# Another hand-written order of all blocks in a fused delta-rule attention and MLP kernel

## The chip, the cores and the metric

The kernel runs on one core of a Trainium2 chip. Its engines are PE (TensorE, matrix multiply; PEld is its weight load), DVE (VectorE), ACT (ScalarE), POOL (GpSimd) and SP (SyncE, whose queue issues most DMAs). The metric is device time in microseconds, taken as the median of several runs. The kernel before took 590.74 us (three runs, 589.99 to 594.02).

## The reference

Four batches of eight heads (32 sequences of 768 steps, head size 48) go through a delta rule, and its result, as 3072 tokens of 384, through a two-layer MLP:

```python
k_n = k / (norm(k) + 1e-6)
for t in range(768):
    y[t]  = q[t] @ state
    v_old = k_n[t] @ state
    state = state + beta[t] * outer(k_n[t], v[t] - v_old)
x = y.transpose(0, 2, 1, 3).reshape(3072, 384)
h = x @ w_in                                  # 384 -> 2048
g = h * tanh(softplus(h))
out = g @ w_out                               # 2048 -> 384
```

q, k, v and beta are float32. The two weight matrices come as 64-bit floats and have to be turned into a high and a low 32-bit part on the chip.

## The kernel before, in words

**Attention.** The 768 steps are cut into 12 chunks of 64 (numbers 0 to 11 in the names). Two chunks make a group g (0 to 5). For each group the Gram products of k (`pg`) come from PE, ACT and DVE write them out (`d`, `at`), DVE turns them into a layout in which a triangular system can be solved (`gt`, L1461), solves it by pairs of products and sums (`pr` L1509, `gt` L1511), and turns the answer back (`d<-gt`, L1531). That last transposition of group g, `d1` for group 1 and so on, releases the products `ta2`, `ta4`, ... on PE (L1641, L1666), with which the even chunk of the group begins. Then the state goes through the chunks in series: `tb`, `pz` and `gq` (old values and products with q), `py` (result), `ps` (new state).

k of the chunks 2 and later is loaded by eight small DMAs for each chunk (`kt2`, `kt3`, `kt4`, ..., 64 KB each, L1237), and DVE transposes it in place (L1409). That transposition waits for all eight DMAs. v is loaded into `vt`, q of the first chunks into `q1`, unturned k into `xx0` and `xx1`.

**MLP.** The tokens of one chunk are one step n of the MLP: eight units `g1.n.0` to `g1.n.7` (18 matmuls each into `h`, L1888; ACT makes `e` and `g` from it in L1903 and L1904, DVE the low part of `g` in L1905) and eight units `g2.n.0` to `g2.n.7` (12 matmuls into `acc`, L1922). These 192 dense units are the filler between the steps of attention.

**Weights.** Twenty-four `ri` and thirty-two `ro` loads bring the weights; each passes through DVE (L1296, L1309, L1313, some in L1304), ACT (L1299, L1317) and, for the low part, PE (`loi`, `loo`) or an accumulating DMA issued by POOL (L1336).

**Order.** Nothing here is left to a scheduler. Each block of work is a generator with a key, and the table `TT` holds a time number for each of its pieces. `run` takes the pieces from a heap by that number and emits their instructions, on all five engines, in this order; each engine then works its own list strictly in order. So a number in `TT` decides behind which instructions another one stands on its engine, and, for loads, its place in the SP queue. `SLOT` says which buffer each tile takes. `warm` is a list of times at which dummy matmuls on a zero tile (L1949) are put on PE. SP's DMAs use eight semaphores in turn: each DMA waits until the eighth one before it has landed.

**What the change touches.** `TT`, `SLOT` and `warm`; `unit`, which copies two identity blocks into `xx0` and `xx1` each (L1220); `gram_out`, which writes out the Gram products of the first two chunks; and `out` in `early`, which does so for the groups.

Of the kernel before, what the change touches and what calls it, by code (L numbers as in the profile page):

```python
# [29 lines left out]
def bcast_in(ap, n):  # L30
# [5 lines left out]
    'loadk0': [0],  # L36
    'warm0.501': [1],
    'loadk1': [2],
    'loadi0': [3],
    'cv0': [4, 81, 110, 135, 139, 150, 151, 165, 1563],  # L40
    'warm43.6': [5],
    'loado1': [6],
    'warm36.4': [7],
    'warm0.602': [8],
    'loadi1': [9],
    'warm11.501': [10],
    'loadb': [11],
    'warm29.5': [12],
    'turn_k(0,0)': [13],
    'turn_k(0,0).0>1': [14],  # L50
    'loado2': [15],
    'turn_k(0,1)': [16],
    'turn_k(0,1).0>1': [17],
    'cv4': [18, 129, 174, 183, 209, 210, 219, 220, 714],
    'loada': [19],
    'early0': [20, 21, 24, 29, 34, 39, 44, 45, 46, 49, 50, 51, 52, 53, 57, 58, 64, 65, 66, 67, 68, 69, 70, 72, 73, 76, 84, 85, 88, 96, 97, 98, 99, 101, 102, 251, 1259],
    'turn_k(1,0)': [22],
    'turn_k(1,0).0>1': [23],
    'early0.2>1': [25],
    'early0.1>1': [26],  # L60
    'turn_k(1,1)': [27],
    'turn_k(1,1).0>1': [28],
    'loadq': [30],
    'early0.0>1': [31],
    'early0.3>1': [32],
    'loadi5': [33],
    'loadv': [35],
    'cv5': [36, 40, 176, 180, 182, 199, 200, 212, 687],
    'turn_beta()': [37],
    'cv1': [38, 55, 105, 133, 134, 145, 146, 167, 997],  # L70
    'loado14': [41],
    'warm11.602': [42],
    'warm12.101': [43],
    'turn_q0(1,)': [47],
    'turn_q0(1,).0>2': [48],
    'loado6': [54],
    'turn_q0(1,).0>1': [56],
    'turn_q0(0,)': [59],
    'warm0.6': [60],
    'warm12.3': [61],  # L80
    'warm11.903': [62],
    'loadi4': [63],
    'scale_v(0,1)': [71],
    'loado3': [74],
    'loadi2': [75],
    'warm11.603': [77],
    'warm11.702': [78],
    'warm0.5': [79],
    'warm12.1': [80],
    'ats_gq[0,1]': [82],  # L90
    'warm11.601': [83],
    'loado8': [86],
    'turn_q0(0,).0>2': [87],
    'warm12.102': [89],
    'warm12.201': [90],
    'warm11.9': [91],
    'warm30.6': [92],
    'warm30.601': [93],
    'turn_q0(0,).0>1': [94],
    'gq00': [95],  # L100
    'loado12': [100],
    'merge1': [103, 124, 270, 271],
    'merge1.0>1': [104],
    'scale_v(0,0)': [106],
    'cv12': [107, 132, 234, 258, 272, 276, 282, 283, 1487],
    'gq00.0>2': [108],
    'merge0': [109, 140, 156, 160],
    'cv2': [111, 112, 161, 162, 164, 166, 168, 202, 1269],
    'loadi9': [113],
    'cv26': [114, 127, 154, 184, 538, 542, 551, 553, 554],  # L110
    'cv8': [115, 148, 273, 274, 294, 295, 305, 306, 881],
    'loado11': [116],
    'loado10': [117],
    'gq00.0>1': [118],
    'cv17': [119, 138, 207, 394, 424, 428, 429, 431, 1435],
    'loado0': [120],
    'warm11.502': [121],
    'warm32.2': [122],
    'warm11.703': [123],
    'warm46.601': [125],  # L120
    'merge1.1>1': [126],
    'cv24': [128, 153, 228, 504, 506, 508, 511, 512, 527],
    'loado13': [130],
    'cv3': [131, 136, 137, 178, 179, 213, 235, 243, 858],
    'loadi3': [141],
    'cv19': [142, 188, 247, 415, 416, 440, 444, 455, 1325],
    'warm12.002': [143],
    'loado9': [144],
    'cv20': [147, 300, 320, 484, 485, 487, 491, 520, 550],
    'cv21': [149, 205, 206, 322, 401, 410, 411, 412, 413],  # L130
    'warm11.503': [152],
    'merge0.0>1': [155],
    'cv9': [157, 158, 175, 238, 252, 253, 254, 257, 1164],
    'merge0.1>1': [159],
    'unit(1,)': [163],
    'cv6': [169, 170, 181, 225, 226, 236, 277, 321, 902],
    'loado4': [171],
    'cv7': [172, 194, 232, 233, 242, 244, 246, 278, 442],
    'cv10': [173, 189, 237, 292, 303, 304, 317, 326, 1459],
    'loado15': [177],  # L140
    'warm40.201': [185],
    'warm11.801': [186],
    'warm12.001': [187],
    'loadi11': [190],
    'warm42.1': [191],
    'warm50.02': [192],
    'cv18': [193, 314, 318, 385, 386, 392, 393, 400, 570],
    'merge0.2>1': [195],
    'merge0.3>1': [196],
    'loado7': [197],  # L150
    'cv13': [198, 309, 327, 332, 340, 349, 354, 356, 1481],
    'ats_a[0,0]': [201],
    'cv27': [203, 316, 324, 325, 530, 543, 544, 545, 546],
    'ats_a[0,1]': [204],
    'cv23': [208, 221, 256, 341, 450, 460, 474, 475, 477],
    'ats_gq[0,1].0>2': [211],
    'warm50.04': [214],
    'ats_a[0,1].0>1': [215],
    'ats_a[0,0].0>1': [216],
    'loadi10': [217],  # L160
    'cv22': [218, 269, 374, 384, 465, 476, 480, 481, 505],
    'ats_b[0,0]': [222],
    'loado5': [223],
    'ats_b[0,0].0>1': [224],
    'ats_b[0,1]': [227],
    'loadi7': [229],
    'loadx': [230],
    'warm50.09': [231],
    'unit(0,)': [239],
    'ats_z[0,0]': [240],  # L170
    'ats_b[0,1].0>1': [241],
    'loadi6': [245],
    'ats_z[0,1]': [248],
    'ats_z[0,0].0>1': [249],
    'cv15': [250, 279, 312, 313, 328, 329, 345, 346, 433],
    'ats_y[0,0]': [255],
    'ats_z[0,1].0>1': [259],
    'cv11': [260, 265, 290, 296, 301, 302, 319, 335, 454],
    'loadp': [261],
    'loadi8': [262],  # L180
    'cv16': [263, 287, 365, 368, 369, 373, 380, 381, 471],
    'ats_gq[0,1].0>1': [264],
    'loads': [266],
    'loadk2': [267],
    'cv14': [268, 281, 289, 336, 337, 358, 359, 360, 1045],
    'merge1.2>1': [275],
    'scale_v(1,0)': [280],
    'merge1.3>1': [284],
    'warm50.11': [285],
    'warm50.13': [286],  # L190
    'warm50.14': [288],
    'scale_v(1,1)': [291],
    'ats_y[0,0].0>1': [293],
    'ats_y[0,1]': [297],
    'ats_s[0,0]': [298],
    'ats_y[0,1].0>1': [299],
    'ats_s[0,0].0>1': [307],
    'turn_q(1,0)': [308],
    'cv25': [310, 366, 367, 446, 497, 498, 503, 510, 523],
    'early1': [311, 361, 362, 364, 395, 397, 399, 405, 406, 408, 420, 421, 422, 425, 426, 434, 435, 436, 437, 438, 439, 445, 447, 449, 451, 461, 462, 464, 466, 467, 472, 473, 486, 488, 489, 493, 494, 495, 496, 499, 509, 515, 516, 517, 518, 519, 528, 529, 534, 535, 536, 537, 540, 547, 548, 549, 560, 561, 562, 563, 565, 571, 572, 573, 574, 575, 576, 580, 581, 587, 588, 598],  # L200
    'g1.0.0': [315],
    'turn_q(1,1)': [323],
    'ats_gq[1,0]': [330],
    'ats_gq[1,0].0>1': [331],
    'g1.0.0.0>1': [333],
    'ats_s[0,1]': [334],
    'ats_a[1]': [338],
    'ats_a[1].0>1': [339],
    'ats_gq[1,0].0>2': [342],
    'g1.0.1': [343],  # L210
    'g1.0.1.0>1': [344],
    'g1.0.1.0>2': [347],
    'g1.0.0.0>2': [348],
    'loadk3': [350],
    'g1.0.1.0>3': [351],
    'g1.0.0.0>3': [352],
    'g1.0.3': [353],
    'early2': [355, 478, 482, 483, 391, 539, 555, 556, 599, 607, 608, 616, 617, 619, 620, 622, 623, 627, 628, 629, 630, 634, 635, 636, 641, 642, 643, 644, 647, 648, 649, 651, 652, 653, 656, 657, 658, 665, 666, 667, 668, 669, 670, 673, 676, 677, 678, 681, 686, 688, 689, 690, 697, 698, 699, 704, 705, 706, 707, 709, 710, 711, 712, 713, 715, 717, 718, 721, 722, 724, 731, 748, 758, 763],
    'ats_s[0,1].0>1': [357],
    'early1.2>1': [363],  # L220
    'ats_b[1]': [370],
    'ats_b[1].0>1': [371],
    'g2.0.0': [372],
    'early1.3>1': [375],
    'ats_z[1,0]+s_gq[1,1]': [376],
    'ats_z[1,0]+s_gq[1,1].0>2': [377],
    'ats_z[1,0]+s_gq[1,1].0>1': [378],
    'g2.0.1': [379],
    'ats_z[1,0]+s_gq[1,1].0>3': [382],
    'ats_z[1,1]': [383],  # L230
    'g1.0.3.0>1': [387],
    'g1.0.3.0>2': [388],
    'g1.0.3.0>3': [389],
    'ats_z[1,1].0>1': [390],
    'early1.4>1': [396],
    'early1.5>1': [398],
    'g1.0.2': [402],
    'g1.0.4': [403],
    'g1.0.2.0>1': [404],
    'ats_s[1,0]': [407],  # L240
    'g1.0.2.0>2': [409],
    'ats_s[1,1]': [414],
    'g1.0.5': [417],
    'g1.0.4.0>1': [418],
    'g1.0.4.0>2': [419],
    'ats_y[1,1]': [423],
    'prep(2,)': [427],
    'g1.0.2.0>3': [430],
    'ats_y[1,0]': [432],
    'g1.0.4.0>3': [441],  # L250
# [808 lines left out]
def kernel(  # L1059
# [43 lines left out]
    C = 64  # L1103
# [1090 lines left out]
```

## Time and profile before

| what | value |
|---|---|
| runs | 594.02, 590.74, 589.99 us; median 590.74 |
| profiled execution | 591.69 us, of which the span of the trace is 590.0 us |
| PE busy | 568.4 us (96% of the span) |
| DVE busy | 399.9 us (68%) |
| ACT busy | 275.8 us (47%) |
| POOL busy | 82.6 us (14%) |
| PEclk in 40 slices | 9879899999999999999999999999999999999999 |
| chain that ended last | PE 63%, DVE 14%, SP queue 9%, DMA 7% |

Busy time says how long an engine had an instruction in work. PE's idle time is the span less its busy time, 21.6 us. PEclk is the granted clock of TensorE in tenths of its full speed (2.4 GHz), and a digit below 9 in the first slices says that it ran partly at the lower level, 1.2 GHz.

### The profile page before, as it was taken

To read this page: it belongs to the slowest core of one execution; us is meant where nothing else is said; L and a number is where in the kernel's file an instruction comes from. 1 tells how busy PE (TensorE), PEld (TensorE's weight loads), DVE (VectorE), ACT (ScalarE), POOL (GpSimd) and SP (SyncE) were. 2 spreads that over 40 slices of the span, in tenths; PEclk is the share of its full clock that TensorE was granted. 3 is DMA by queue.
4 is the path that set the end of the run, shared out by engine and by line. 5 is a ranking of instruction groups with operands and counts; after the bars stand their busy time and mean duration, and the time that the engine had idled before them with its cause. 6 is when DMAs were issued, how large, how long until landed. Compare 5 with 4: busy or idle time off the path is not lost.

```text
span 590.0 us, 22753 instructions
## 1 busy us (share of the span) xinstructions
PE 568.4 (96%) x9985; PEld 530.3 (90%) x9994; DVE 399.9 (68%) x881; ACT 275.8 (47%) x538; POOL 82.6 (14%) x144
## 2 busy tenths in 40 slices
PE   7879899999999999999999999999999999999997
PEld 4446689998999989999999999999999999999996
DVE  2898899997998658996659995557996343432101
ACT  3358788645533445343645334444424543253222
POOL 5101322324102200102101003101001310000000
PEclk9879899999999999999999999999999999999999
DMA  8898894852322423332434214122111231110011
GB/s 210 248 356 218 127 158 75 133 92 56 53 41 55 64 32 67 53 56 42 63 57 81 32 36 64 18 50 53 16 42 30 42 72 27 29 29 1 0 28 28
DMA packets 161779, 43.27 MB, mean 73 GB/s; under 512 B 149008, under 2 KB 157664, under 8 KB 161680
## 3 DMA queue, kind: packets, MB, share of 16 engines
q1 hardware_dynamic: 156640, 36.93, 31.4%
q0 software_dynamic: 2784, 4.29, 4.2%
q8 instruction: 79, 1.29, 0.9%
q10 hardware_dynamic: 2256, 0.59, 0.5%
q14 instruction: 20, 0.16, 0.1%
HBM read 32.87 MB, written 4.72 MB: 64 GB/s over the span
## 4 chain that ended last, share of the span: by engine, by line
PE 63%; DVE 14%; SPq 9%; DMA 7%; ACT 3%; issue 2%; POOL 0%; DVEq 0%; ACTq 0%; POOLq 0%
PE acc L1922 26%; PE h L1888 24%; SPq L1237 9%; DMA ro<-in_moe_w_out_dram 4%; DVE gt L1511 3%; PE py L1641 3%; DVE pr L1509 3%; PE pz L1641 3%; PE gq L1641 2%; DVE g L1905 2%; PE ps L1641 1%; PE pg L1641 1%; DVE d L1531 1%; PE ta L1666 1%; DMA kn<-in_k_dram 1%
## 5 line engine op out<-in xcount | busy, mean ns | idle before, releaser
L1922 PE MATMUL acc<-wo,g 128*128 128x384 f32 x1152 | 214.2, 338 | 0.4 <-DVE g L1905 0.2
L1888 PE MATMUL h<-x,wi 128*128 128x256 f32 x1728 | 211.0, 279 | 0.6 <-ACT e L1903 0.3
L1888 PEld LDWEIGHTS h<-x,wi 128*128 128x128 f32 x1728 | 204.2, 188 | 2.9 <-DVE x L1792 0.6
L1922 PEld LDWEIGHTS acc<-wo,g 128*128 128x128 f32 x1152 | 197.5, 188 | 3.4 <-DVE g L1905 1.3
L1903 ACT ACTIVATE e<-h 128x512 f32<-128x512 f32 x96 | 57.2, 598 | 138.4 <-PE h L1888 103.8
L1905 DVE TENSOR_TENSOR g<-e,g 128x512 fp32r<-128x512 f32 x96 | 65.6, 691 | 77.5 <-ACT g L1904 77.1
L1904 ACT CAST g<-e 128x512 fp32r<-128x512 f32 x96 | 58.8, 621 | 19.0 <-PE acc L1922 17.1
L1511 DVE TENSOR_TENSOR gt<-gt,pr 128x58 f32<-128x58 f32 (+9 forms) x164 | 55.7, 339 | 4.7
L1509 DVE TENSOR_TENSOR pr<-gt 128x58 f32<-128x58 f32 (+9 forms) x164 | 55.4, 338 | 4.3
L1641 PE MATMUL gq<-xx,kt 48*64 48x112 f32 (+1 forms) x768 | 50.1, 266 | 0.6 <-issue 0.6
L1641 PEld LDWEIGHTS pz<-vt,tt 64*64 64x64 f32 x768 | 43.5, 135 | 6.0 <-ACT tt L1721 1.5
L1641 PE MATMUL pz<-vt,tt 64*64 64x48 f32 x768 | 47.4, 226 | 0.9 <-ACT tt L1721 0.9
L1641 PEld LDWEIGHTS gq<-xx,kt 48*64 48x64 f32 x768 | 43.8, 132 | 1.8 <-issue 1.5
L1550 POOL COPY tt<-d 32x512 f32<-32x512 f32 x40 | 26.5, 661 | 102.7 <-DVE d L1531 62.0
L1745 DVE TENSOR_TENSOR xx<-gq,amask 64x256 f32<-64x256 f32 x96 | 40.1, 418 | 0.7
L1742 DVE TENSOR_TENSOR vt<-vt,gq 128x192 f32<-128x192 f32 x44 | 15.5, 352 | 34.6 <-PE tb L1666 13.2
L1619 POOL TENSOR_TENSOR vt<-vt,ne 128x384 f32<-128x384 f32 x24 | 20.8, 870 | 114.9 <-DMA vt<-in_v_dram 113.1
L1770 ACT COPY xx<-pz 64x384 f32<-64x384 f32 x48 | 22.7, 474 | 29.3 <-PE gq L1641 20.7
L1626 DVE STREAM_TRANSPOSE xx<-xx 128x1024 f32<-128x1024 f32 x20 | 24.8, 1240 | 5.6 <-DMA xx<-in_q_dram 4.6
L1641 PE MATMUL py<-xx 128*32 128x64 f32 (+1 forms) x1536 | 26.9, 224 | 0.5 <-ACT xx L1770 0.5
L1641 PEld LDWEIGHTS py<-xx 128*32 128x32 f32 (+1 forms) x1536 | 22.9, 109 | 4.9 <-issue 2.8
L1792 DVE TENSOR_TENSOR x<-py,x 128x384 fp32r<-128x384 f32 x24 | 13.2, 554 | 13.9 <-ACT x L1791 13.6
(163 smaller groups left out, 609.4 us busy)
## 6 DMA issues: line engine op xcount, KB each, us to landing
ri<-in_moe_w_in_dram SPq DMA_DIRECT2D x24, 256.0 KB, 4.9
ro<-in_moe_w_out_dram SPq DMA_DIRECT2D x32, 192.0 KB, 4.7
kt<-in_k_dram SPq DMA_DIRECT2D x76, 64.0 KB, 3.4
vt<-in_v_dram SPq DMA_DIRECT2D x48, 96.0 KB, 3.1
xx<-in_k_dram SPq DMA_DIRECT2D x48, 96.0 KB, 3.0
out_dram<-o SPq DMA_DIRECT2D x46, 96.0 KB, 2.2
xx<-in_q_dram SPq DMA_DIRECT2D x80, 32.0 KB, 2.2
wo<-mo POOLq DMA_DIRECT2D x9, 192.0 KB, 3.4
```

Source lines behind the costliest of these rows:

```text
L1237: m = (nc.scalar if turns[0] else nc.sync).dma_start(out=dst, in_=src)
L1509: nc.vector.tensor_tensor(out=pv, in0=nj, in1=xj, op=ALU.mult)
L1511: nc.vector.tensor_tensor(out=below, in0=below, in1=pv, op=ALU.add)
L1550: nc.gpsimd.tensor_copy(out=tt2[r, t2, :, c0:c0 + 32], in_=dts[g][r, t2])
L1626: nc.vector.transpose(x, x)
L1641: last[:] = [nc.tensor.matmul(*a, start=True, stop=True)]
L1745: nc.vector.tensor_tensor(out=x[r, p4, hh, D:D + C], in0=ps[r, :, d:], in1=bcast_mid(amask[r], 4), op=ALU.mult)
L1888: nc.tensor.matmul(h[:, f2, :], wt["i", f * P // WI * NCH + c][:, i2, f0:f0 + P], x[:, c, :], start=(i == 0), stop=(i == 3 * NCH - 1))
L1903: for d, f in ((0.7, lambda: nc.scalar.activation(e, h, AF.Mish)), (0.7, lambda: nc.scalar.copy(out=gg[:, 0], in_=e)), (0.8, lambda: nc.ve ...
L1904: (0.7, lambda: nc.scalar.copy(out=gg[:, 0], in_=e)),
L1905: (0.8, lambda: nc.vector.tensor_tensor(out=gg[:, 1], in0=e, in1=gg[:, 0], op=ALU.subtract))):
L1922: nc.tensor.matmul(acc[t], gg[:, a, f2, t * P:(t + 1) * P], wt["o", f][:, i2, :], start=(f == 0 and a == i2 == 0), stop=(f == NF - 1 and a ...
```

## The change

All numbers of `TT` are replaced by others, and so is the table of buffers `SLOT`, which follows from it. The list `warm` has 27 entries in place of 37 (53 dummy matmuls for 71). The identity blocks are copied by POOL instead of DVE. In `gram_out` and, from group 1 on, in `out`, DVE's instruction is emitted behind ACT's; none is added or removed. The new code lines stand a few lines higher, so L1409 of before is L1400 in the change, L1237 is L1228, and so on. Apart from the four copies and the 18 dummy matmuls each engine has the same instructions as before, in another order. The two loads of beta go out on ACT's queue ahead of ACT's part of the k loads.

```diff
 TT = {
...
-    'loadb': [11],
+    'unit(0,)': [0],
+    'loadb': [1],
...
-    'unit(1,)': [163],
+    'unit(1,)': [34],
...
-    'early2.6>1': [569],
+    'early2.6>1': [555],
...
-              warm=[(0.5,2),(0.501,2),(0.6,2),(0.602,1),(11.501,2),...,(50.13,2),(50.14,2)],
+              warm=[(0.501,2),(11.501,2),(11.502,2),(11.503,2),...,(60.08,2),(60.17,2)],
...
     def unit(h):
         for hh in range(2):
             r = slice(64 - 64 * hh, 128 - 64 * hh)
-            nc.vector.tensor_copy(xx[h][r, :, hh, D + C:], bcast_mid(ident[r, r.start:r.start + D], PB))
+            nc.gpsimd.tensor_copy(xx[h][r, :, hh, D + C:], bcast_mid(ident[r, r.start:r.start + D], PB))
         give(f"U{h}")
...
     def gram_out(n, ps, to, at):
         nc.scalar.mul(out=to, in_=ps[:, :, 0:32], mul=sign(1))
+        nc.scalar.activation(at, ps[:, :, 0:32], AF.Copy, scale=sign(0))
         nc.vector.scalar_tensor_tensor(to, ps[:, :, 32:], sign(2), to, op0=ALU.mult, op1=ALU.add)
-        nc.scalar.activation(at, ps[:, :, 0:32], AF.Copy, scale=sign(0))
...
-                    to = dt[:, t2, pr, :]
-                    nc.vector.tensor_tensor(out=to, in0=ps[:, :, 32:],
-                                            in1=bcast_mid(lmask, 8), op=ALU.mult)
+                    def block():
+                        nc.vector.tensor_tensor(out=dt[:, t2, pr, :], in0=ps[:, :, 32:],
+                                                in1=bcast_mid(lmask, 8), op=ALU.mult)
+
+                    if not g:
+                        block()
                     if fused(n):
                         nc.scalar.activation(at[:, pr, :], ps[:, :, 0:32], AF.Copy, scale=sign(0))
                     else:
                         nc.scalar.copy(out=at[:, pr, :], in_=ps[:, :, 0:32])
+                    if g:
+                        block()
```

What the tables do to the engines shows in the lists of instructions. The first place is the SP queue from the last weights to v of chunk 2 (`ri`, `ro` weights; `q1`, `kt`, `vt`, `xx` as above; x8 means eight DMAs in a row). Before:

```order
L1237 DMA vt1_0_1083<-in_v_dram 64x8x48 x2
L1237 DMA vt1_1_1086<-in_v_dram 64x8x48 x2
L1237 DMA ri8_1089<-in_moe_w_in_dram 128x512 x2
L1237 DMA q1_1096<-in_q_dram 32x16x32 x8
L1237 DMA kt2_1105<-in_k_dram 32x16x32 x8
L1237 DMA xx0_100<-in_k_dram 64x8x48 x2
L1237 DMA kt3_1435<-in_k_dram 32x16x32 x8
L1237 DMA kt4_1469<-in_k_dram 32x16x32 x8
L1237 DMA xx1_101<-in_k_dram 64x8x48 x2
L1237 DMA vt2_0_1963<-in_v_dram 64x8x48 x2
```

The same queue in the change:

```order
L1228 DMA ri8_963<-in_moe_w_in_dram 128x512 x2
L1228 DMA ri7_973<-in_moe_w_in_dram 128x512 x2
L1228 DMA ro13_1042<-in_moe_w_out_dram 128x384 x2
L1228 DMA q1_1047<-in_q_dram 32x16x32 x8
L1228 DMA kt3_1105<-in_k_dram 32x16x32 x8
L1228 DMA kt2_1216<-in_k_dram 32x16x32 x8
L1228 DMA vt1_0_1250<-in_v_dram 64x8x48 x2
L1228 DMA vt1_1_1253<-in_v_dram 64x8x48 x2
L1228 DMA xx0_100<-in_k_dram 64x8x48 x2
L1228 DMA xx1_101<-in_k_dram 64x8x48 x2
L1228 DMA kt4_1425<-in_k_dram 32x16x32 x8
L1228 DMA vt2_0_1877<-in_v_dram 64x8x48 x2
```

The weights end earlier, `vt1` has gone from ahead of the last weight to behind `kt2`, and `xx1` from behind `kt4` to ahead of it. Counted from the start of the queue, the last load of `kt4` is the 112th in place of the 110th.

The second place is DVE's list around the transposition of `kt4`. Before, it stands behind the products that end chunk 1's `gq` (`vt1`, `xx1`):

```order
L1450 TENSOR_TENSOR d1_1488<-pg2_1_1525,lmask_87 128x256
L1742 TENSOR_TENSOR vt1_1_1086<-vt1_1_1086,gq1_10_1618 128x192
L1745 TENSOR_TENSOR xx1_101<-gq1_10_1618,amask_88 64x4x64 x2
L1742 TENSOR_TENSOR vt1_1_1086<-vt1_1_1086,gq1_11_1635 128x192
L1745 TENSOR_TENSOR xx1_101<-gq1_11_1635,amask_88 64x4x64 x2
L1309 TENSOR_SCALAR ri10_916<-ri10_916 128x512
L1313 SCALAR_TENSOR_TENSOR mo9_1692<-ro9_708 128x384
L1905 TENSOR_TENSOR g0_3_1466<-e0_3_1465,g0_3_1466 128x512
L1409 STREAM_TRANSPOSE kt4_1469<-kt4_1469 128x1024
L1313 SCALAR_TENSOR_TENSOR spare_107<-ro8_471 128x384
L1450 TENSOR_TENSOR d1_1488<-pg3_0_1706,lmask_87 128x256
```

In the change it stands ahead of them:

```order
L1901 TENSOR_TENSOR g0_0_1350<-e0_0_1349,g0_0_1350 128x512
L1901 TENSOR_TENSOR g0_2_1504<-e0_2_1503,g0_2_1504 128x512
L1300 TENSOR_SCALAR ro8_942<-ro8_942 128x384
L1400 STREAM_TRANSPOSE kt4_1425<-kt4_1425 128x1024
L1300 TENSOR_SCALAR ro13_1042<-ro13_1042 128x384
L1441 TENSOR_TENSOR d1_1443<-pg2_1_1509,lmask_87 128x256
L1304 SCALAR_TENSOR_TENSOR mo9_1609<-ro9_615 128x384
L1738 TENSOR_TENSOR vt1_1_1253<-vt1_1_1253,gq1_10_1614 128x192
L1741 TENSOR_TENSOR xx1_101<-gq1_10_1614,amask_88 64x4x64 x2
L1901 TENSOR_TENSOR g0_1_1323<-e0_1_1322,g0_1_1323 128x512
L1738 TENSOR_TENSOR vt1_1_1253<-vt1_1_1253,gq1_11_1631 128x192
L1741 TENSOR_TENSOR xx1_101<-gq1_11_1631,amask_88 64x4x64 x2
```

Twelve instructions that stood ahead of the transposition (nine of them in these rows) now stand behind it. One, the low part `g0_2`, has gone the other way, and one that stood between it and `d1`'s end, the low part `g1_0`, has gone behind that.

The third place is the head of POOL's list: `ym0` is a buffer of zeros, `gt0` belongs to group 0's solve, `vt0` is v of chunk 0. Before:

```order
L1226 MEMSET tt2_104 32x32x32 x2
L1348 MEMSET ym0_108 128x32x16
L1496 MEMSET gt0_329 128x32
L1619 TENSOR_TENSOR vt0_1_341<-vt0_1_341,ne0_367 128x384
L1619 TENSOR_TENSOR vt0_0_338<-vt0_0_338,ne0_367 128x384
```

In the change:

```order
L1339 MEMSET ym0_108 128x32x16
L1211 COPY xx0_100<-ident_84 64x8x48 x2
L1211 COPY xx1_101<-ident_84 64x8x48 x2
L1492 MEMSET gt0_324 128x32
L1615 TENSOR_TENSOR vt0_0_359<-vt0_0_359,ne0_376 128x384
```

The four copies fill POOL's list between `ym0` and `gt0`.

## Rows read from the trace of the kernel before

**Rows 1.** Windows, with columns PE, PEld, DVE, ACT, POOL busy, PEclk, DMA, GB/s.

```profile
50.00:75.00 25.00, 22.55 (x587) 16.83 (x589) 20.58 (x44) 20.19 (x43) 6.63 (x8) 0.93 0.77 145
75.00:100.00 25.00, 23.86 (x586) 22.28 (x585) 23.46 (x51) 21.25 (x39) 5.27 (x15) 1.00 0.73 122
```

**Rows 2.** Waits of PE up to 68 us: us in total, times, longest.

```profile
PE ma L1569 <- DVE tu L1522: 4.3, 1, 4.3
PE loi L1325 <- DVE spare L1313: 1.9, 1, 1.9
```

**Rows 3.** Waits of PE from 68 us to the end.

```profile
PE pz L1641 <- ACT tt L1721: 0.9, 2, 0.7
PE ta L1666 <- DVE d L1531: 0.7, 2, 0.6
```

**Rows 4.** Waits of DVE from 33 to 140 us.

```profile
DVE ri L1296 <- DMA ri<-in_moe_w_in_dram: 2.9, 1, 2.9
```

**Rows 5.** Timeline of the SP queue: start, us, what, count.

```profile
63.23 6.02 SPq L1237 DMA_DIRECT2D kt<-in_k_dram  x8
...
70.73 14.17 SPq L1237 DMA_DIRECT2D kt<-in_k_dram  x16
85.00 1.29 SPq L1237 DMA_DIRECT2D xx<-in_k_dram  x2
```

**Rows 6.** The kt loads of SP between 60 and 90 us: duration, starts, landing.

```profile
L1237 SPq DMA_DIRECT2D kt<-in_k_dram x24: 400/574/1942, 63.2 to 83.4; - x24
...
DMA to landing us min/median/max: 2.6/4.5/5.8
```

**Rows 7.** Timeline of DVE around the transposition of kt4.

```profile
87.00 0.35 DVE L1742 TENSOR_TENSOR vt<-vt,gq 128x192 f32<-128x192 f32 x1
87.28 0.85 DVE L1745 TENSOR_TENSOR xx<-gq,amask 64x256 f32<-64x256 f32 x2
...
89.65 0.55 DVE L1313 SCALAR_TENSOR_TENSOR mo<-ro 128x384 int32<-128x384 int32 x1
90.49 0.69 DVE L1905 TENSOR_TENSOR g<-e,g 128x512 fp32r<-128x512 f32 x1 [0.29 <-ACT g L1904]
91.10 1.24 DVE L1409 STREAM_TRANSPOSE kt<-kt 128x1024 f32<-128x1024 f32 x1
```

**Rows 8.** Timeline of DVE: the transposition that ends group 1's solve.

```profile
136.73 2.08 DVE L1531 STREAM_TRANSPOSE d<-gt 128x1024 f32<-128x1024 f32 x1
```

**Rows 9.** Windows of DVE from kt4's end to d1's, and to d2's.

```profile
92.34:138.81 46.47, 44.54 (x106) 1.00 0.55 90
138.81:190.00 51.19, 45.93 (x108) 1.00 0.31 54
```

**Rows 10.** Timeline of PE: the first product behind group 1's solve.

```profile
138.96 1.20 PE L1641 MATMUL ta<-d,at 32*32 32x32 f32 x64 [0.21 <-DVE d L1531]
```

**Rows 11.** Timeline of PE: a dense unit, and the first product behind group 2's solve.

```profile
186.90 2.20 PE L1888 MATMUL h<-x,wi 128*128 128x256 f32 x18
...
190.01 0.25 PE L1666 MATMUL ta<-d,at 64*33 64x32 f32 x4 [0.56 <-DVE d L1531]
```

**Rows 12.** Windows of 1 us around PE's two longest waits, columns as rows 1.

```profile
30.00:31.00 1.00, 0.00 (x0) 0.00 (x0) 0.97 (x2) 0.00 (x0) 0.00 (x0) 0.50 1.01 375
...
36.00:37.00 1.00, 1.00 (x65) 0.74 (x64) 0.94 (x4) 0.20 (x1) 0.00 (x0) 0.69 1.04 371
...
64.00:65.00 1.00, 1.00 (x2) 0.00 (x0) 1.00 (x2) 0.87 (x2) 1.00 (x2) 0.50 0.70 107
...
67.00:68.00 1.00, 1.00 (x33) 0.95 (x33) 1.00 (x3) 0.96 (x2) 0.00 (x0) 0.83 0.75 109
```

**Rows 13.** The identity copies of DVE: duration min/median/max, first and last start.

```profile
L1220 DVE COPY xx<-ident x4: 351/354/357, 42.4 to 55.4; 64x384 f32<-64x384 f32 x4
```

**Rows 14.** Timeline of POOL: its first instruction of the solve, with the gap before.

```profile
20.89 0.16 POOL L1496 MEMSET gt<- 128x32 f32 x1 [11.75 <-DVE gt L1493]
```

**Rows 15.** The page: POOL's copies of another block, count, busy, mean ns.

```profile
L1550 POOL COPY tt<-d 32x512 f32<-32x512 f32 x40 | 26.5, 661 | 102.7 <-DVE d L1531 62.0
```

**Rows 16.** Timeline of DVE in group 0's solve, while POOL scales v.

```profile
22.16 0.78 DVE L1511 TENSOR_TENSOR gt<-gt,pr 128x72 f32<-128x72 f32 x1
```

## What the change will do to the time

> **What bounds the kernel now.** I began with busy time. PE works 568.4 of the 590.0 us of the span, so no order of the same blocks can win more than its 21.6 idle us, and the question is only where PE stands idle. The windows say where to look: PE is short of work early, and DVE has next to no idle time from 50 to 100 us, with 23.46 of 25 us busy in the second of these windows [rows 1]. Next come PE's waits. Up to 68 us the longest is 4.3 us, for the end of group 0's solve on DVE, and the next 1.9 us [rows 2]; after that the largest sums are 0.9 and 0.7 us [rows 3]. The reader should see that PE hardly waits later because its list always brings a dense unit when attention isn't ready. So two things decide the time: when DVE finishes each group's solve, and how much PE work stands ahead of the product that waits for it. In the timelines both are tight for group 1: its last transposition starts at 136.73 and lasts 2.08 us, so it ends at 138.81 [rows 8], and PE's first product behind it begins at 138.96 after a wait of 0.21 us [rows 10]. Group 2 looks the same, with a wait of 0.56 us at 190.01 [rows 11]. Between kt4's transposition, which ends at 92.34 (91.10 and 1.24) [rows 7], and 138.81 DVE is busy for 44.54 of 46.47 us, with 106 instructions [rows 9]: the rest is the step from one instruction to the next. DVE alone sets that stretch.
>
> **The change part by part.**
>
> *The head.* DVE loses its four identity copies, 0.35 us each, 1.4 us in all [rows 13], and the wait of 2.9 us for the late weight [rows 4], since that weight is loaded earlier and `vt1` later. Ahead of kt4's transposition DVE has the twelve instructions less that went behind it and one more, `g0_2`. Eight of the twelve are of the kinds of rows 7, four `xx1` and two `vt1` products, one shift-and-combine and one low part; the others are a second low part, half a `d` and two shifts. From the steps between their starts they come to 5.1 us, and `g0_2` to 0.6 us (0.69 [rows 7] less the overlap with the next). So DVE would reach the transposition at 91.10 - 5.1 - 1.4 + 0.6 - 2.9 = 82.3 us, 8.8 us sooner.
>
> *kt4's loads.* They are not sooner. The last one was issued at 83.4, and such loads land 2.6 to 5.8 us later, 4.5 in the median [rows 6], so it landed between 86.0 and 89.2 and was never waited for. Now it is the 112th load of the queue where it was the 110th. The SP queue has no gap there: 8 loads took 6.02 us, 16 took 14.17, and the pair for `xx1` took 1.29 [rows 5]. Two more loads ahead cost 1.3 us, which makes 87.3 to 90.5 us. I take 89.0, the middle. DVE, in order, then stands still from about 82 to 89 us, and all that it gained in the head is gone.
>
> *From kt4 to d1.* Behind the transposition the twelve instructions are added, 5.1 us; `g0_2` (0.6) and `g1_0` (0.6), which moved behind `d1`, are taken away. The stretch is 46.47 + 3.9 us. So group 1's solve ends at 89.0 + 1.24 + 46.47 + 3.9 = 140.6 us, where it was 138.81: **1.8 us later**.
>
> *PE at that point.* I counted the dense units in PE's list ahead of this product: 22 before, 21 now. One unit is 2.20 us, 2.1 without its overlap [rows 11]. PE comes there earlier by that and by up to 2.9 us from the head, at 133.7 to 136.6 us, and must wait 4 to 7 us. The unit that it lacks has to be done afterwards: **2.1 us**.
>
> *The clock.* After the wait of 4.3 us, PE's granted clock was 0.50, that is 1.2 GHz, from before its end at 31.75 until 36.3 (0.69 in the window that begins at 36); after the wait of 1.9 us it was 0.50 from 64 to 67 and 0.83 in the next window [rows 2, 12]. That is 4.5 and 3.2 us at half speed, a loss of 2.3 and 1.6 us of work. The wait at d1 is as long as the longer one, but dense work lies ahead of it, so the loss could also be nothing. I take **1.6 us**. Should the clock drop after the shorter waits of the head too, this is hidden in the wait at d1. The Trainium skill, "TensorE: Matmul & The Clock Gate", section "What's actually happening", puts the ramp penalty under 1% of a typical span; an estimate from that page, 5.9 us here, would make the sum 599.7.
>
> *From d1 on.* DVE's work from d1 to d2 grows by `g1_0`, 0.6 us, on a stretch of 51.19 us [rows 9]. The PE work between is the same, so PE, late by the clock's loss, no longer waits there: **-0.6 us** [rows 11]. At the later solves PE has about one unit less ahead as well, which is the same unit and not a second one. The attention work of the last chunk comes later, behind six more dense units, but still ahead of dense work, so I cost it at nothing; the cover is those units.
>
> *Small edits.* The GpSimd copies: by its copies of another block 0.66 us each [rows 15], 2.6 us in all, in a gap of 11.75 us [rows 14]: nothing. Below that lies a gain of the 1.4 us on DVE already counted; above it, blocked VectorE work. An instruction of the solve took 0.78 us while GpSimd scaled v [rows 16]. The Trainium skill, "SBUF — State Buffer", section "Who interferes with whom", says that a VectorE instruction with two inputs in SBUF is blocked by a GpSimd one that reads SBUF. If each copy delayed the first solve by its whole length, 2.6 us would be lost, and the 7 us that DVE waits for kt4 cover it. The 18 dummy matmuls less lie in waiting time. The swap of ACT and DVE in `gram_out` and `out` moves one step of under a microsecond on either side of a full queue: nothing, with the same cover. Beta's loads ahead of k on ACT's queue delay the first solve by a few us at most: same cover again.
>
> **The sum.** 1.8 + 2.1 + 1.6 - 0.6 = 4.9 us. The profiled execution took 591.69 us, 1.7 more than its span; it stands 0.95 above the median of the runs, to which I add the sum: 590.74 + 4.9 = **595.6 us**.
>
> **The rivals.**
>
> *The loads come in time (chance 0.17).* If the small loads land as fast as the quickest of them and the weights ahead of them end sooner, DVE finds kt4 there. For it: 393 KB of loads that stood ahead of `q1` now stand behind it. Against it: 24 kt loads and their landing times show no slack [rows 5, 6]. PE then keeps the 2.9 us of the head, and d1 is ready before PE comes: 590.74 - 2.9 = 587.8 us.
>
> *The two ends cancel (0.13).* kt4 lands near 86 us, d1 ends some 1 us early, PE waits 2 us, its clock stays up: the missing unit and the early end come out at 590 to 591.5 us.
>
> *The loads come later (0.20).* This is the one on the other side of 1%. SP issued 16 loads in 14.17 us, 0.89 each, against 0.75 in the eight before them [rows 5]. If the 24 loads from `kt2` to `kt4` all go at the slow pace, 24 x 0.14 = 3.4 us are added at kt4, microsecond for microsecond at d1, and the long wait costs 2.3 us of clock and not 1.6. That gives 595.6 + 3.4 + 0.7 = 599.7 us. It decides from a landing at 90.0 on, where the sum passes 596.6.
>
> **How the numbers follow.** A measurement of this kernel can tell about 1% from no change, 5.9 us: 584.8 and 596.6 are the bounds. My forecast has 0.50; its own range goes from 592 (kt4 at 87.3 and no clock loss: 595.6 - 1.7 - 1.6 = 592.3) to 598 (kt4 at 90.5 and 2.3 us of clock: 597.8). About a third of it, 0.16, lies above 596.6. With the last rival's 0.20, less a little of it that stays below, slower has 0.34. Faster needs 6 us of PE's 21.6 idle us, most of which lie in the head and ahead of the loads: 0.05, out of the first rival. The rest, 0.61, is no change. The range from 587.5 to 600.5 takes in all four cases but the tails of the outer two.
>
> **What would show it.** In the profile after: DVE idle for 4 to 8 us ahead of kt4's transposition (L1400), put down to a DMA or to issue; that transposition at 88 to 90.5; d1 (L1527) ending at 139 to 142; PE waiting 4 to 7 us for it and a granted clock of 0.50 behind it; hardly a wait at d2. If DVE does not stand at kt4, or PE comes to d1 without waiting, the forecast is wrong and the first rival holds. If PE loses its time at other places, most of all behind 200 us, I have misread where the orders differ.

## The result, and the profile after

Beside 11 runs of the kernel before (median 590.99 us, 588.73 to 594.02), 11 runs of the change took 597.64 us in the median (594.47 to 601.99): a ratio of **1.0126, 95% interval 1.0105 to 1.0146**, 6.65 us slower. The profiled execution of the change took 599.48 us with a span of 597.8; it lies 1.8 us above its median, so its span is 7.8 us longer than the one before, while the medians differ by 6.65.

By the bounds that the prediction set itself (1%, 596.6 us) this is slower, to which it gave 0.34; it had given 0.61 to no change.

The PE waits of the change, first up to 68 us and then from there on, answer to [rows 2, 3]:

```profile
PE ma L1565 <- DVE tu L1518: 7.4, 1, 7.4
...
PE acc L1918 <- DVE g L1901: 3.2, 2, 2.2
PE pg L1435 <- issue: 1.7, 1, 1.7
PE gq L1637 <- issue: 1.4, 2, 0.8
PE ta L1637 <- DVE d L1527: 0.5, 1, 0.5
```

The forecast wait of 4 to 7 us at `d1` is not there, 0.5 us is. In its place stand waits that the kernel before had not: for a Gram product (`pg`) and, much later, for low parts of `g`. The wait of 7.4 us is no later solve: PE's first product behind group 0's solve begins at 30.19 us instead of 31.75, and PE had only run out of other work sooner. DVE's largest waits from 33 to 142 us, as [rows 4]:

```profile
DVE kt L1400 <- DMA vt<-in_v_dram: 3.0, 1, 3.0
DVE mi L1304 <- DMA wo<-mo: 2.3, 1, 2.3
```

DVE's timeline shows where they lie, and what became of [rows 7, 8]. The last number in brackets is the idle time before the instruction:

```profile
75.68 1.25 DVE L1400 STREAM_TRANSPOSE kt<-kt 128x1024 f32<-128x1024 f32 x1 [2.95 <-DMA vt<-in_v_dram]
...
83.27 0.69 DVE L1304 SCALAR_TENSOR_TENSOR mi<-ri 128x512 int32<-128x512 int32 x1 [2.35 <-DMA wo<-mo]
...
87.76 1.24 DVE L1400 STREAM_TRANSPOSE kt<-kt 128x1024 f32<-128x1024 f32 x1
...
138.63 2.05 DVE L1527 STREAM_TRANSPOSE d<-gt 128x1024 f32<-128x1024 f32 x1
```

The first is `kt2`, the third `kt4`, which DVE takes without any wait; the last ends at 140.68 us. (The rows name `vt` for the first wait, the load that stands behind `kt2` in the queue; the last load of `kt2` went out at 71 us at the latest, and such loads land 3.1 to 4.5 us later, about when the wait ends.) The SP queue answers to [rows 5], and the row of the kt loads between 76 and 92 us to [rows 6]:

```profile
60.19 10.77 SPq L1228 DMA_DIRECT2D kt<-in_k_dram  x16
71.01 4.13 SPq L1228 DMA_DIRECT2D vt<-in_v_dram  x4
75.23 2.93 SPq L1228 DMA_DIRECT2D xx<-in_k_dram  x4
78.27 6.47 SPq L1228 DMA_DIRECT2D kt<-in_k_dram  x8
```

```profile
L1228 SPq DMA_DIRECT2D kt<-in_k_dram x8: 486/592/1787, 78.3 to 84.1; - x8
...
DMA to landing us min/median/max: 3.1/3.9/4.5
```

The first 16 loads are `kt3` and, behind it, `kt2`; then come `vt1` and `xx1`; the last eight are `kt4`. By these rows its last load landed between 87.2 and 88.6 us (84.1 and 3.1 to 4.5), and by 87.76, since DVE began then without a wait. POOL's timeline says why `mi7` was late at 83.27:

```profile
77.21 0.98 POOL L1615 TENSOR_TENSOR vt<-vt,ne 128x384 f32<-128x384 f32 x1 [5.43 <-DMA vt<-in_v_dram]
78.14 1.73 POOL L1552 COPY tt<-tt 32x512 f32<-32x512 f32 x2
79.81 0.86 POOL L1327 DMA_DIRECT2D wo<-mo  x1
```

POOL stands 5.43 us at the scaling of `vt1`. Behind that, in its list, is the accumulating DMA from `mo7`, for which ACT had done its part by 72.57 us. DVE's `mi7` takes the buffer of `mo7` and has to wait until that DMA has landed (3.4 us at the quickest, which makes 83.2).

On PE the late `kt2` gives a wait, and then a stretch at the lower clock. PE's timeline, and windows of 1 us (columns as rows 1):

```profile
77.02 2.33 PE L1435 MATMUL pg<-kt 48*32 48x64 f32 x64 [1.66 <-issue]
79.29 4.21 PE L1884 MATMUL h<-x,wi 128*128 128x256 f32 x18
...
140.74 1.20 PE L1637 MATMUL ta<-d,at 32*32 32x32 f32 x64 [0.52 <-DVE d L1527]
```

```profile
46.00:47.00 1.00, 1.00 (x12) 0.43 (x11) 1.00 (x4) 0.70 (x3) 0.00 (x0) 0.80 0.94 269
50.00:51.00 1.00, 1.00 (x29) 0.94 (x24) 1.00 (x3) 0.23 (x1) 0.00 (x0) 0.50 0.96 297
56.00:57.00 1.00, 1.00 (x30) 0.91 (x30) 1.00 (x4) 0.22 (x1) 0.00 (x0) 0.58 1.05 192
...
76.00:77.00 1.00, 0.00 (x0) 0.01 (x1) 1.00 (x2) 0.00 (x0) 0.00 (x0) 1.00 0.64 113
77.00:78.00 1.00, 0.98 (x27) 0.94 (x31) 1.00 (x2) 0.47 (x1) 0.79 (x1) 0.66 0.70 125
78.00:79.00 1.00, 1.00 (x48) 1.00 (x38) 1.00 (x3) 0.38 (x2) 1.00 (x2) 0.50 0.88 146
...
84.00:85.00 1.00, 1.00 (x66) 0.91 (x60) 1.00 (x3) 1.00 (x4) 0.00 (x0) 0.92 1.19 200
```

The dense unit at 79.29 lasts 4.21 us where one lasts 2.20 [rows 11]. From 77.3 to 84.2 us (by the shares in the first and the last of these windows) PE works at 1.2 GHz without a pause, and half of these 6.8 us, 3.4 us of work, is lost. It is not the only such stretch that is new: from 46.6 to 56.8 us, by the shares of the first windows, PE works at 1.2 GHz too, 10.2 us or 5.1 us of work, where the kernel before has 1.00. Behind `d1` the clock is 1.00.

**Where the 7.8 us are.** PE's first product behind `d1` began at 138.96 us [rows 10], now at 140.74: **1.78 us**. The rest, 6.02 us, lies behind it. PE alone from that product to the end, before and after (columns: length, PE busy, PEclk, DMA, GB/s):

```profile
138.96:590.00 451.04, 444.51 (x7306) 1.00 0.25 42
```

```profile
140.74:597.80 457.06, 447.24 (x7318) 1.00 0.24 42
```

PE is busy for 2.7 us more (the one dense unit, 2.1, that is no longer done ahead, and 0.6 that no row assigns) and idle for 9.82 us instead of 6.53, **3.3 us** more. Nearly all of that is two waits, at 266.6 and 414.9 us, 2.21 and 0.97 us long:

```profile
268.85 3.07 PE L1918 MATMUL acc<-wo,g 128*128 128x384 f32 x16 [2.21 <-DVE g L1901]
```

```profile
415.84 0.98 PE L1918 MATMUL acc<-wo,g 128*128 128x384 f32 x4 [0.97 <-DVE g L1901]
```

The first is for the low part of `g3_6`, which stands in DVE's list between the last products of group 3's solve. Rows of DVE there:

```profile
264.43 0.30 DVE L1507 TENSOR_TENSOR gt<-gt,pr 128x130 f32<-128x130 f32 x1
264.76 0.78 DVE L1505 TENSOR_TENSOR pr<-gt 128x108 f32<-128x108 f32 x1
265.58 0.80 DVE L1507 TENSOR_TENSOR gt<-gt,pr 128x108 f32<-128x108 f32 x1
266.30 1.23 DVE L1622 STREAM_TRANSPOSE xx<-xx 128x1024 f32<-128x1024 f32 x1
...
268.11 0.68 DVE L1901 TENSOR_TENSOR g<-e,g 128x512 fp32r<-128x512 f32 x1
```

ACT delivered `g3_6` at 264.7; DVE came to it at 268.11. In between it also lost about 1 us in the two products of 0.78 and 0.80 us. So of the step from `d1` to the end, two parts were forecast (the unit, no wait at `d2`) and one, these waits, was not.

### The profile page after: what moved, and what is told of

Read it like the earlier page. It is cut to its first block, busy times and chain, and to the rows that moved or that the text cites. A ratio compares the mean times of both kernels' runs of the same rounds, so it can differ in the third digit from the quotient of the medians.

```text
span 597.8 us, 22729 instructions
## 1 busy us (share of the span) xinstructions
PE 571.6 (96%) x9970; PEld 534.4 (89%) x9976; DVE 403.1 (67%) x877; ACT 274.5 (46%) x538; POOL 86.1 (14%) x148
## 4 chain that ended last, share of the span: by engine, by line
PE 56%; DVE 19%; issue 2%; DMA 1%; ACT 1%; POOL 0%; SPq 0%; DVEq 0%; ACTq 0%; POOLq 0%
PE acc L1918 24%; PE h L1884 20%; DVE pr L1505 5%; DVE gt L1507 4%; PE py L1637 3%; PE pz L1637 3%; DVE g L1901 3%; PE gq L1637 2%; PE ps L1637 1%; PE pg L1637 1%; DVE xx L1827 1%; DVE xx L1741 1%; PE ta L1662 1%; DVE xx L1622 1%; DVE gt L1457 1%
## 5 line engine op out<-in xcount | busy, mean ns | idle before, releaser
L1901 DVE TENSOR_TENSOR g<-e,g 128x512 fp32r<-128x512 f32 x96 | 67.9, 713 | 78.6 <-ACT g L1900 78.3
L1507 DVE TENSOR_TENSOR gt<-gt,pr 128x58 f32<-128x58 f32 (+9 forms) x164 | 57.3, 349 | 4.9
L1738 DVE TENSOR_TENSOR vt<-vt,gq 128x192 f32<-128x192 f32 x44 | 15.4, 351 | 20.2 <-PE tb L1662 7.5
```

What stands on the lines that cost most here:

```text
L1507: nc.vector.tensor_tensor(out=below, in0=below, in1=pv, op=ALU.add)
L1901: (0.8, lambda: nc.vector.tensor_tensor(out=gg[:, 1], in0=e, in1=gg[:, 0], op=ALU.subtract))):
```

## The experiments

My theory from this profile had two parts: in front, DVE's gain is eaten by the late `kt2` and `mi7` and not by `kt4`; behind 200 us, the new order has waits of its own. The rival for the front was the forecast's own step (the place of `kt4`); the rival for the back was that everything comes from the front. In the diffs a line is a piece of work in the order of emission; `early2[1]` is the transposition of `kt4`.

Beside e1 to e4, e5 to e8 and e9 to e12 ran the kernel before, with medians of 589.75, 589.84 and 590.44 us; brackets give the ratio and its 95% interval. The buffers of `SLOT` were not assigned anew in e3 to e12.

**Front and back apart.** e1 has the change's order for the first 680 blocks and the order of before for the others; e2 the reverse.

```diff
 e1:  order[0:680]
-  before
+  change
 e2:  order[680:]
-  before
+  change
```

> First 680 blocks in the order of the change, all later ones in the order of before. Theory A (the ends of the solves on VectorE set the time, in the front because of late loads, in the back because of solve 3): only the front's loss is left, some 4 us, so about 595 us against 591 of before, with the end of solve 1 near 140.7 us. Rival (the later order alone does the harm, the head's loss is made good): about 591 us. Rival (the head alone does it, clock and all): about 597.5 us, as the change.

> First 680 blocks in the order of before, all later ones in the order of the change. Theory A: the back's share of the loss, 3 to 4 us, so 594 to 595 us, with a wait of PE for the low part of g shortly before the end of solve 3 and that solve ending later than 268.6 us. Rival (the head alone does it): 591 us. Rival (the back alone does it): 597.5 us.

e1 took 598.5 us (1.0136, 1.0097 to 1.0175), e2 604.06 (1.0238, 1.0187 to 1.0288). Both missed their forecasts, and together they lose far more than the change does: each has a seam of its own. In e1 PE waits where the orders meet, for the end of solve 2; in e2, there and later, for ACT's `e`:

```profile
195.20 0.25 PE L1665 MATMUL ta<-d,at 64*33 64x32 f32 x4 [1.79 <-DVE d L1530]
```

```profile
PE h L1892 <- ACT e L1907: 4.9, 4, 2.0
```

Not all of e2's waits belong to the seam: one, of 1.97 us until 260.85, stands shortly before the end of solve 3, where the change waits as well. So the shares of front and back can't be read from the times of these two. What they do show is in the table further down: with the order of before behind block 680 the stretch from `d2` to `d3` is 78.9 us, with the change's order 83.1.

**The late kt2.** e3 loads `kt2` ahead of `kt3`. e4 also puts the transposition of `kt4` back behind the `gq` products of chunk 1.

```diff
+loadk2
 loadk3
...
-loadk2
```

```diff
-early2[1]
 cv15[4]
...
 ats_z[1,0]+s_gq[1,1].0>3
+early2[1]
```

> The change with the eight loads of kt2 ahead of those of kt3. VectorE's wait of 2.95 us before it transposes kt2, PE's of 1.66 us and the half clock behind it (3.2 us) go. Theory A: VectorE then only reaches kt4's transposition sooner and waits there, since kt4's last load lands at 87.2 us and the transposition starts at 87.76 now: solve 1 ends at most 0.5 us earlier, PE waits for it, time 597 us (597.6 now). Rival B (PE's lost clock in the head is the loss): 4 us less, about 593.5 us.

> As the one with kt2 first, and kt4's transposition moved back behind the products that end chunk 1's gq, where it stood before the change. Theory A: nothing on VectorE waits for kt4 any more, solve 1 ends 2.5 to 3 us earlier (near 138 us), time about 595 us, 2 to 3 us below the one with kt2 first alone. Rival B: no more than the one with kt2 first alone.

e3 took 598.94 us (1.0132, 1.0076 to 1.0188): nothing was won. Theory A had that, but not its reason: DVE doesn't wait at `kt4`. `kt2` was turned at 70.84 us, 4.8 sooner, and DVE then waited for POOL's scaling of `vt1`:

```profile
DVE vt L1741 <- POOL vt L1618: 4.9, 1, 4.9
DVE mi L1307 <- DMA wo<-mo: 3.0, 2, 2.7
```

PE's wait did not go either: it is 2.9 us now, for the `xx` behind that `vt`, and the granted clock is 0.50 from 79.6 us on. So e3 does not test what the half clock in the head is worth.

e4 took 596.72 us (1.0101, 1.0065 to 1.0136), the best of the change's variants, with an interval that overlaps the change's own. In it `d1` ends 47.2 us behind `kt4`'s transposition instead of 51.7: the instructions past which it was moved are worth 4.5 us, of 5.1 forecast for the twelve. PE's wait before the end of solve 3 is still there, 1.9 us at 262.

**kt4's place and the late weight alone.** e5 is the kernel before with `kt4`'s transposition moved ahead as in the change; e6 is the kernel before with the late weight `ri8` loaded ahead of `vt1`.

```diff
+early2[1]
 early1.3>1
...
-early2[1]
```

```diff
+loadi8
 loadp
-loadi8
```

> The kernel before with one block moved: kt4's transposition stands ahead of the last product of chunk 2's Gram block and of chunk 1's gq, as in the change, nothing else is changed. Theory A (in order, VectorE stands at kt4 until its last load lands near 88.6 us, and what stood ahead of it comes afterwards): VectorE idle some 2 us ahead of kt4, solve 1 ends at 140 to 141 us instead of 138.8, time 592 to 593 us against 591 of before. Rival (kt4's place costs nothing): 591 us and solve 1 at 138.8 us.

> The kernel before with the load of the weight ri8 ahead of the loads of v of chunk 1. VectorE's wait of 2.9 us and PE's of 1.9 us at 61 us go. Theory A: VectorE keeps up to 2.5 us of it (kt4 is transposed 2.5 us after its last load landed), solve 1 ends near 136.5 us, PE comes earlier too, time 588 to 589 us. Rival (a gain in the head is lost again at the next load): 591 us.

e5 took 590.1 us (1.0008, 0.9989 to 1.0027), e6 589.8 (1.0000, 0.9979 to 1.0020): neither makes a difference, as the rivals had it. In e5 DVE finds `kt4` landed, although it comes to it 5.4 us sooner than before:

```profile
85.08 0.68 DVE L1308 SCALAR_TENSOR_TENSOR ri<-ri 128x512 f32<-128x512 f32 x1
85.68 1.24 DVE L1413 STREAM_TRANSPOSE kt<-kt 128x1024 f32<-128x1024 f32 x1
```

The condition of theory A, a late landing, wasn't there in this execution. The same 16 loads of `kt3` and `kt4` took 11.21 us in the SP queue, where they took 14.17 in the profile before [rows 5]:

```profile
69.34 11.21 SPq L1241 DMA_DIRECT2D kt<-in_k_dram  x16
```

With the loads in the same order e12 has 11.26 us: the pace of the queue differs between executions.

In e6 the wait of 2.9 us for the weight [rows 4] is gone, and a wait of the same kind has come at the next load, `kt2`:

```profile
70.42 1.25 DVE L1413 STREAM_TRANSPOSE kt<-kt 128x1024 f32<-128x1024 f32 x1 [3.29 <-DMA xx<-in_k_dram]
```

**The wait at 266 us.** e7 is e4 with ACT's and DVE's steps for `g3_6` ahead of five pieces of the solve. e8 is e7 with a dense unit, `g1.4.2`, ahead of `ta6` and two low parts of step 7 sooner.

```diff
 g1.3.5.0>2
+g1.3.6.0>2
 early3[46]
 early3[47]
+g1.3.6.0>3
...
 g2.3.5
-g1.3.6.0>2
...
-g1.3.6.0>3
```

```diff
 g1.4.1.0>3
+g1.4.2
 ats_z[5,0]+s_gq[5,1]+s_a[6]
...
-g1.4.2
...
 early5[9]
+g1.7.1.0>3
...
 g1.7.2
+g1.7.2.0>3
...
-g1.7.2.0>3
...
-g1.7.1.0>3
```

> The kernel with kt2 first and kt4 back, and the two steps on ScalarE and VectorE that make g of unit 6 of step 3 moved ahead in their lists, so that PE's wait of 2 us for it shortly before the end of solve 3 goes. Theory A (the end of solve 3 on VectorE sets the time there): PE waits at solve 3 instead, time 596 to 597 us, as without it. Rival C (PE's wait for g is the loss of the back): 594.5 to 595 us.

> As e7_g3_6_early, and one dense unit (unit 2 of step 4) moved ahead of the product that waits for solve 3, and the two low parts of g for which PE waits 1 us at 415 us moved ahead on VectorE. Theory A: the unit fills the wait for solve 3, 2 us less, and 1 us less at 415: 593.5 us. Rival C: 1 us less than e7_g3_6_early and no more.

e7 took 600.29 us (1.0171, 1.0120 to 1.0222) and e8 601.51 (1.0200, 1.0162 to 1.0237). The edit failed: `g` has three buffers here, none was free so early, ACT stood 5.14 us until PE gave one back, DVE 3.28 us behind ACT, and the wait doubled (rows of e7):

```profile
262.39 0.69 DVE L1904 TENSOR_TENSOR g<-e,g 128x512 fp32r<-128x512 f32 x1 [3.28 <-ACT g L1903]
```

```profile
PE acc L1921 <- DVE g L1904: 4.0, 1, 4.0
```

**vt1 and kt2 both first.** e9 is the change with both loads ahead of `kt3`; e10 is e9 with the dense unit `g2.3.4` ahead of `g1.4.1`, so that a buffer of `g` is freed sooner; e11 is e10 with e8's second edit.

```diff
 cv15[0]
+loadp
+loadk2
 loadk3
...
-loadk2
...
-loadp
```

```diff
 early3[55]
+g2.3.4
 g1.4.1
...
-g2.3.4
```

> The change with the loads of v of chunk 1 and of kt2 moved ahead of those of kt3, nothing else. Theory D (GpSimd, in order, waits 5.4 us for v of chunk 1; the accumulating DMA of wo7 behind it goes out late and VectorE waits 2.3 us for the buffer that it reads; with the 3 us at kt2 this delays solve 1): both waits go, solve 1 ends near 136.5 us instead of 140.7, time 593.5 to 594.5 us, some 4 us less than the change. Rival C (the loss lies behind 180 us, and the head's waits are covered): 597 us.

> As e9_vt1_kt2_first, and on PE the dense unit g2.3.4 ahead of g1.4.1, so that one of the three buffers of g comes free before ScalarE needs it for unit 6 of step 3. PE's wait of 2.2 us for g near 266 us goes. Theory A (the end of solve 3 on VectorE sets the time there): PE waits for solve 3 instead, same time as e9 within 1 us. Rival C: 2 us less than e9.

> As e10_g2_3_4_ahead, one more dense unit (g1.4.2) ahead of the product that waits for solve 3, and the low parts g7_1 and g7_2 ahead on VectorE, for which PE waits 1 us at 415 us. Theory A: the unit fills the wait for solve 3 and the wait at 415 goes, 3 us less than e10, about 591 us. Rival C: 1 us less than e10.

They took 598.15 us (1.0151, 1.0108 to 1.0193), 598.92 (1.0147, 1.0120 to 1.0174) and 600.29 (1.0172, 1.0133 to 1.0212). In e9 the waits at `kt2` and at POOL are gone and the one at `mi7` is 0.6 us. Now comes the wait that the forecast had named:

```profile
87.16 1.25 DVE L1403 STREAM_TRANSPOSE kt<-kt 128x1024 f32<-128x1024 f32 x1 [5.38 <-DMA kt<-in_k_dram]
```

In e10 it is 2.81 us and in e11 7.7 us (the row names `vt`, the next load in the queue). There PE waits 5.6 us for the products behind that transposition:

```profile
DVE kt L1403 <- DMA vt<-in_v_dram: 7.7, 1, 7.7
```

```profile
PE pg L1438 <- DVE d L1444: 5.6, 1, 5.6
```

My theory for the front, that the time comes back once `kt2` and `mi7` are in time, fell with e9. Nor did e10 take away the wait before the end of solve 3, 1.8 us in it: ACT delivers `g3_6` at 261.53 us and DVE comes to it at 264.36, so the place in DVE's list holds it and not the buffer. What this wait costs differs from one execution to the next: the 16 matmuls behind it take 3.07 us in the change, and in e10 4.49, since the clock fell there (the window has the columns of rows 1):

```profile
265.10 4.49 PE L1921 MATMUL acc<-wo,g 128*128 128x384 f32 x16 [1.83 <-DVE g L1904]
```

```profile
267.00:268.00 1.00, 1.00 (x5) 1.00 (x4) 0.97 (x2) 0.29 (x1) 0.00 (x0) 0.50 0.00 0
```

Behind the same wait they take 3.06 us in e4 and e9 and 4.57 and 4.58 in e11 and e3. The second edit of e8 and e11 did what it was made for, the wait near 415 us is gone in both, and no time was won.

**The copies alone.** e12 is the kernel before with the four identity copies on GpSimd, at the head of its list.

```diff
-            nc.vector.tensor_copy(xx[h][r, :, hh, D + C:], ...)
+            nc.gpsimd.tensor_copy(xx[h][r, :, hh, D + C:], ...)
```

> The kernel before with the four identity copies on GpSimd, first in its list, nothing else. VectorE has 1.4 us less work at 42 and 55 us, GpSimd works some 2.6 us in a gap of 11.75 us. Theory: VectorE's saved time is waited for the late loads again, 589 to 590 us against 590 of before. Rival (VectorE's work in the head sets the time): 588.5 us. Rival (the copies block VectorE's first instructions): 592 us.

It took 589.76 us (0.9986, 0.9971 to 1.0001): no loss, and a gain of at most 0.3%, not clear of no change. The change's copies took 0.50 to 0.64 us each on POOL, from 9.2 us on, and nobody waited for them.

**The profiles side by side.** Ends in us of `kt4`'s transposition and of the solves 1 to 3, each the start of that transposition and its duration from the timelines of DVE:

| kernel | kt4 end | d1 | d1 - kt4 | d2 | d3 | d3 - d2 |
|---|---|---|---|---|---|---|
| before | 92.34 | 138.81 | 46.5 | 189.95 | 268.56 | 78.6 |
| e5 | 86.92 | 138.03 | 51.1 | 189.16 | 266.94 | 77.8 |
| e6 | 91.15 | 137.61 | 46.5 | 188.72 | 267.37 | 78.7 |
| e12 | 90.47 | 136.94 | 46.5 | 188.06 | 266.80 | 78.7 |
| e1, front of the change | 87.39 | 138.02 | 50.6 | 195.14 | 274.08 | 78.9 |
| change | 89.00 | 140.68 | 51.7 | 192.16 | 273.80 | 81.6 |
| e3 | 89.25 | 139.93 | 50.7 | 191.03 | 272.37 | 81.3 |
| e4, kt4 put back | 89.25 | 136.42 | 47.2 | 187.88 | 269.10 | 81.2 |
| e7, from e4 | 93.36 | 140.05 | 46.7 | 191.19 | 276.00 | 84.8 |
| e8, from e7 | 91.57 | 138.80 | 47.2 | 190.00 | 275.05 | 85.1 |
| e9 | 88.41 | 141.01 | 52.6 | 192.46 | 272.89 | 80.4 |
| e10 | 87.63 | 138.24 | 50.6 | 189.20 | 269.95 | 80.8 |
| e11 | 90.65 | 142.27 | 51.6 | 193.65 | 274.82 | 81.2 |
| e2, back of the change | 91.64 | 138.09 | 46.5 | 190.10 | 273.22 | 83.1 |

Two things repeat. Wherever the transposition stands ahead of its twelve instructions, `d1` follows 50.6 to 52.6 us behind it; where it stands behind them, 46.5 to 47.2. And every kernel with the change's order behind block 680 needs 80.4 to 83.1 us from `d2` to `d3` (e7 and e8 with their doubled wait 85), the others 77.8 to 78.9. With the change's front and `kt4` where the change has it, the first column lies between 87.4 and 90.7 us, whatever waits come ahead. In e4 `d1` is 2.4 us sooner than before and the run still slower: what it gains at `d1` it loses behind it.

Each row is one execution, and `d1` varies among rows with the same order up to solve 3: 138.2 to 142.3 us in e9, e10 and e11, 136.4 to 140.1 in e4, e7 and e8. A step of 2 us in that column alone is not clear of this. The stretch behind it is clearer. The span less `d1` is 450.4 to 451.2 us in the four kernels with the order of before (before, e5, e6, e12), and 455.8 to 460.5 in the change and e3, e4, e9, e10 and e11 (459.8 and 462.1 in e7 and e8). So at least 4.6 us of the loss lie behind `d1` in every one of these profiles, with the 2.1 us of the unit that is no longer done ahead among them.

## Why the prediction was right or wrong

The forecast time, 595.6 us, is 2 us short, and the sign and place of the first terms hold. One step failed, one was missing. Up to `d1` the sum has 1.8 us, measured 1.8; behind it 3.1 (2.1, 1.6 and -0.6), measured 6.0.

*Right: the end of solve 1.* Forecast at 140.6 us, 1.8 later; measured at 140.68. That it fits so closely is luck: two errors of about 1.2 us cancel in it: `kt4` was turned by 89.00 us and not by 90.2, and the stretch behind it is 51.68 us and not 50.4. The window that answers to [rows 9]:

```profile
89.00:140.68 51.68, 48.65 (x117) 1.00 0.55 91
```

DVE's work in it grew by 4.1 us (3.9 forecast), its idle time by 1.1.

*Right: one dense unit fewer ahead*, 2.1 us (12 matmuls more stand behind that product, 7318 for 7306); and no wait is left at `d2`, as forecast.

*Failed: "DVE, in order, then stands still from about 82 to 89 us".* DVE lost the time before it came to `kt4`. From the start of the span to that transposition its work and its idle time changed like this (DVE alone, before and after):

```profile
0.00:91.10 91.10, 71.44 (x175) 0.93 0.89 216
```

```profile
0.00:87.76 87.76, 64.95 (x159) 0.84 0.89 219
```

The work that I summed was there, 6.5 us less for 5.9 forecast, but the idle time rose by 3.2 us where I had it fall by 2.9. I took away the wait of 2.9 us without asking what is late next: `vt1` and `kt2` had moved behind `kt3` in the SP queue. That made 2.95 us at `kt2` and 2.35 at `mi7`, 5.3 of the 6.1 us between the two; the rest lies in small waits. I had noted that `vt1` is loaded later, and had not looked at who waits for it (POOL) and what is queued behind that (a DMA that frees DVE's buffer). `kt4`'s loads, taken at 89.0, were there by 87.76: their pace came from one execution with a slow queue, and the 24 kt loads took 17.2 us here, 20.2 before. e9 shows that they are indeed the next bound, at nearly the same time.

*Failed in place: the clock.* 1.6 us were forecast behind `d1`. The clock fell at 46.6 and at 77.3 us, the second time behind the wait for `kt2`, which alone cost 3.4 us of work; PE still came to `d1` with 0.52 us to spare, so this didn't delay that product. The prediction had allowed for this case. The Trainium skill, "TensorE: Matmul & The Clock Gate", section "What's actually happening", puts the ramp penalty under 1% of a typical span. The stretch from 77.3 us alone, 3.4 of 597.8 us or 0.6%, agrees; all stretches together don't, since the mean granted clock of the whole execution is 0.976 (0.988 before), idle time included, which is 2.4% of the span. (With that page's estimate the prediction's sum is 599.9, not 599.7.)

*Missing: the back.* 3.3 us of idle PE behind 140.74 us, 3.2 of it in waits for low parts of `g`. I had counted dense units at the solves' ends and not followed the low parts of `g` in DVE's list through solve 3. No experiment took the wait away without bringing another, so that it alone costs this much isn't shown. The forecast named this as the sign of a misreading, and it is one.

So the profile's 7.8 us are 1.8 (`d1`), 2.1 (the unit), 3.3 (waits behind) and 0.6 (not assigned), against 1.8, 2.1, 1.6 and -0.6 forecast. The rival of later loads is out in this profile: `kt4` landed by 87.76 us, not from 90.0 on. So is the one of loads in time: DVE did find `kt4` there, but `d1` was not sooner. And the 21.6 us of PE's idle time are no strict bound for a gain, since its busy time has stretches at 1.2 GHz.

What stays open: how the loss divides between front and back in the median, since both splices bring waits of their own (the profiles put most of it behind `d1`); and which moved pieces make `d2` to `d3` 2 to 4 us longer; of the 3.0 us in this profile 2.4 are DVE's busy time (64.4 us for 62.0), the two slowed products among them. No variant of the change came down to the time before, so the cause of the loss behind `d1` is read from the profiles and not shown by removing it.

## What to carry to other kernels

On an engine that works in order and is fed by a full DMA queue, a removed wait can come back at the next load that is late, as it did in e6 and e9; price the gain by that load, and ask of each load that moved back who waits for it and what is queued behind that one. When a whole order is replaced, compare the waits stage by stage to the end, and not only at the chain that bounds the first stage. A splice of two orders has a seam, and its loss is not a share of either. And a term that rests on the pace of a queue in one execution needs the spread of that pace beside it.

## What the runs showed of the hardware

- **A wait and the clock.** After 1.66 us of idle PE at 75.4 us, the granted clock fell to 0.50 at 77.3, when PE was already at work again, and stayed there for 6.8 us. After 2.21 us at 266.6 us it stayed at 1.00. In e7, with 4.0 us from 263.1 on, it fell at 266.7, while PE still waited, and was back at 270.1. In e10, with 1.83 us from 263.3 on, it fell at 266.3, behind the same kind of dense matmuls as in the change. So neither the length of the wait nor the kind of work directly ahead of it (narrow products of 48 by 64 in the first case, dense matmuls in the others) told whether the clock fell.
- **VectorE beside GpSimd.** Two products of solve 3, each with two inputs in SBUF, took 0.78 and 0.80 us, where their neighbours take 0.30. GpSimd was scaling v just then:

```profile
264.43 0.98 POOL L1615 TENSOR_TENSOR vt<-vt,ne 128x384 f32<-128x384 f32 x1 [20.43 <-DVE pr L1505]
...
265.42 0.82 POOL L1615 TENSOR_TENSOR vt<-vt,ne 128x384 f32<-128x384 f32 x1
```

Each product ended 0.13 to 0.14 us behind GpSimd's instruction (265.54 behind 265.41, 266.38 behind 266.24). The Trainium skill, "SBUF — State Buffer", section "Who interferes with whom", says that such a VectorE instruction contends with a GpSimd one that reads SBUF; these rows agree, and give the price as about 0.5 us for each, less than the 0.98 and 0.82 us of GpSimd's instructions.
- **A DMA behind compute.** In GpSimd's list a DMA stood behind compute: 5.43 us of standing at `vt1` held back an accumulation that was ready at 72.57 us until 79.81, and with it an instruction of VectorE by 2.35 us.
